# One q unit per step between k and G, tile 4 transposed by DMA, q weights loaded ahead of x of tile 8

## The chip, the core and the metric

The kernel runs on one core of one Trainium2 chip. The metric is the device time of one execution in microseconds (us), lower is better; before the change the median of three runs was 113.4 us, from 112.97 to 113.63 us. A core has five engines with instruction streams of their own: TensorE (PE, matrix products, with the loading of its weights shown apart as PEld), VectorE (DVE), ScalarE (ACT), GpSimd (POOL) and SyncE (SP), which here does nothing but start DMA transfers. Matrix products write into PSUM, which the kernel uses as eight banks of 512 float32 columns.

## The reference

The input x has 2048 rows of 640 values. It is normalised by rows, and three terms are added: x itself, a linear attention with 32 heads of 20 columns, and a small expert block that acts on eight selected rows.

```
xn = (x - mean(x)) / sqrt(var(x) + 1e-5)
q, k, v = split(xn @ wqkv)                      # each 2048 x 640, 32 heads of 20
phi(t) = where(t > 0, t + 1, exp(t)) + 1e-6
kv = phi(k)^T v   and   z = sum of phi(k)       # per head
attention = (phi(q) kv / (phi(q) z)) @ wo
r = xn @ w_r;  idx = the 8 largest of r
expert = (silu(xn[idx] @ w_gate) * (xn[idx] @ w_up)) @ w_down * sigmoid(r[idx])
out = x + attention + xn + scatter(expert at idx)
```

## The kernel before, in words

The rows are cut into 16 tiles of 128. The order of every instruction is the order in which the program emits it; no planner moves anything. Each engine runs its own instructions in that order and waits where an operand isn't ready, so a late operand holds up all that stands behind it on the same engine.

For each tile t the front half of the kernel does the following:

- `stat` computes statistics of two halves of 320 columns on DVE (L180) and merges them (L182). `root_pool` (L191, L192, on POOL) or `root_act` (L186, L187, on ACT) makes the reciprocal root.
- `norm_dve` (L201) or `norm_pool` (L208, L212) writes the normalised tile `xn`.
- The transposed tile `xnT` is made in one of two ways: `tr_pe` transposes on PE with five products (L231), and `tr_ev` copies the result out of banks 7 and 6 with one instruction on ACT (L237) and one on DVE (L242); or `tr_dma` has SP start a transposing DMA (L245). Before, tiles 0 to 4 go by PE and tiles 5 to 15 by DMA.
- `k_half` (L253) multiplies the tile by the k weights, five products of 320 columns per half, into banks 0 and 1 (tiles 1 and 2 use banks 2, 3 and 4, 5). `k_act` (L267, L268) takes exp and relu of both halves on ACT, and one column for the router (L270). `k_phi` (L275, DVE) joins them into `pk`.
- `g1` (L282) adds the tile's part of the matrix G = xn^T phi(k) into banks 2 to 6, five products of 512 columns. It runs four tiles behind k.

The q side works in 20 units, each 128 columns of q for a block of four tiles: `q_mm` (L290, five products of 512 columns, bank 7 unless another is named), `q_act` (L299, L300, ACT), `q_phi` (L306, DVE). `q_ev` is the last two. Units 0 to 4 need tiles 0 to 3, units 5 to 9 need tiles 4 to 7. Units 0 to 7 are spread over the front half by the table `q_at`; the rest fill the back half.

The loads of x, of the q weights `wq` and all DMA transposes are started by SP, in program order, on one queue. The large expert weights are started by ACT in steps 6, 8, 10 and 12 (`w_jobs`, L106). `adds` has POOL scale x for the sum at the end (L480, L223).

After the 16 tiles the router finds its eight rows, G is turned into one matrix M per head group and multiplied into `wo` (`kv_mm`, `m_unit`), the remaining q units run, and `o_mm` (L809) makes the output tile by tile.

Of the kernel before, what the change touches and what calls it, by code (L numbers as in the profile page):

```python
# [36 lines left out]
def kernel(  # L37
# [56 lines left out]
    def load_rest():  # L94

        G.memset(x_sb[0:1, 3, 0:1], 0.0)
        SP.dma_start(x_sb[:, 3, :], x_v[:, 3, :])
        for a in (4, 6):
            SP.dma_start(x_sb[:, a : a + 2, :], x_v[:, a : a + 2, :])
        SP.dma_start(x_sb[:, 8:12, :], x_v[:, 8:12, :])  # L100
        for lo, hi in ((0, 3), (3, 5)):
            SP.dma_start(wq[:, lo:hi, :], wqkv_v[:, lo:hi, 0:D])
        SP.dma_start(x_sb[:, 12:16, :], x_v[:, 12:16, :])
# [158 lines left out]
    def k_act(t):  # L262
        b0 = K_BANK.get(t, 0)
        e = evk.tile([P, 2, HW], BF16, tag="ek", name=f"ek{t}")
        r = evk.tile([P, 2, HW], BF16, tag="rk", name=f"rk{t}")
        for b in range(2):
            A.activation(e[:, b, :], ps[:, b0 + b, 0:HW], AF.Exp)  # L267
            A.activation(r[:, b, :], ps[:, b0 + b, 0:HW], AF.Relu)  # L268
        if t:
            A.copy(r_all[:, t : t + 1], ps[:, b0 + 1, HW : HW + 1])  # L270
        kev[t] = e, r
# [121 lines left out]
    def stats2(t):  # L393
        stat(t, 0)
        stat(t, 1)
# [36 lines left out]
    stats2(4)  # L432
    root_pool(4)
    norm_dve(3)
# [18 lines left out]
    tr_dma(5)  # L453
    norm_pool(6)
    tr_dma(6)
    k_phi(0)
# [3 lines left out]
    q_mm(0)  # L460
    k_phi(2)
    k_half(4, 0)
    q_act(0)
    k_half(4, 1)
    k_act(4)
    k_phi(3)
# [6 lines left out]
    q_phi(0)  # L473
    q_mm(1)
    g1(0)
    k_phi(4)
    q_ev(1)
# [6 lines left out]
    q_at = {5: (2, 3), 6: (4,), 8: (5,), 10: (6,), 12: (7,)}  # L484
    later = {12: [const_grep], 13: [copy_grep]}
    add_at = {7: (0, 1), 9: (1, 1), 11: (2, 1), 12: (3, 2), 13: (5, 2), 14: (7, 3), 15: (10, 3)}
    for t in range(5, T):
        qs = q_at.get(t, ())
# [405 lines left out]
```

## Time and profile before

| | |
|---|---|
| median of three runs | 113.4 us |
| time of the profiled execution | 113.12 us |
| its span in the trace | 111.4 us |
| PE busy | 106.1 us, 95% of the span |
| DVE busy | 81.7 us, 73% |
| ACT busy | 64.9 us, 58% |
| POOL busy | 46.7 us, 42% |
| granted TensorE clock over the span | 0.997 |

The span runs from the first to the last instruction in the trace; 1.7 us of the execution lie around it. A product's shown duration is longer than the pace at which products follow each other, because they are pipelined: a product of 512 columns is shown with 379 ns, and five of them in a row take 1.08 us on the chain. The chain of work that ended last is followed back from the last instruction, so a stretch in which the chain holds only PE rows without a break is one in which PE alone sets the time. In timelines the first column is the start and the second the length, both in us; in rows of DMA issues the last number is the time from issue to landing.

### The profile page before, as it was taken

Reading aid. Unit: us, or ns where it says so; the run is one execution under the profiler, and the core shown is the slowest. Engines: PE = TensorE matmul, PEld = TensorE weight load, DVE = VectorE, ACT = ScalarE, POOL = GpSimd, SP = SyncE. Lnnn points to the kernel's source line nnn. Section 1 sums busy time; section 2 is a strip of 40 time slices with the busy share of each in tenths; the row PEclk is TensorE's granted clock in tenths of the full one; section 3 lists DMA queues with packets and bytes.
Section 4 is the critical chain, followed back from the end, with each engine's and each line's share of the span. In section 5 each row is a group of like instructions: output and inputs, shape, how many; then the busy total and the mean of one; then the engine's idle time right before and its main releaser. Section 6 shows DMA issues by size and latency. Waiting matters only on the chain.

```text
span 111.4 us, 2508 instructions
## 1 busy us (share of the span) xinstructions
PE 106.1 (95%) x911; PEld 62.4 (56%) x911; DVE 81.7 (73%) x176; ACT 64.9 (58%) x165; POOL 46.7 (42%) x93
## 2 busy tenths in 40 slices
PE   5899999999999999999999999999999999999990
PEld 2246544545555555655436879635445566777760
DVE  1799799899997987833829444597788888865670
ACT  1459989597767676766019454478997556300000
POOL 6903578370888689999991331000700000000000
PEclk9999999999999999999999999999999999999998
DMA  3989959502899699799999999927929993333333
GB/s 76 325 260 313 363 198 71 100 15 59 246 295 253 173 178 341 129 397 294 221 315 364 385 381 320 298 81 225 245 16 369 363 328 114 118 121 120 121 118 121
DMA packets 27351, 24.59 MB, mean 221 GB/s; under 512 B 8258, under 2 KB 26058, under 8 KB 27338
## 3 DMA queue, kind: packets, MB, share of 16 engines
q1 hardware_dynamic: 21808, 17.45, 56.1%
q10 hardware_dynamic: 5498, 6.97, 18.8%
q8 instruction: 7, 0.11, 0.5%
q14 instruction: 6, 0.05, 0.2%
q0 software_dynamic: 32, 0.01, 0.1%
HBM read 15.93 MB, written 6.56 MB: 202 GB/s over the span
## 4 chain that ended last, share of the span: by engine, by line
PE 80%; ACT 7%; DVE 3%; POOL 2%; DMA 2%; issue 2%; POOLq 0%; ACTq 0%
PE ps L809 19%; PE ps L290 18%; PE ps L282 14%; PE ps L253 14%; PE ps L528 4%; DMA x_sb<-in_A_x_dram 2%; ACT rq L300 2%; PE ps L650 2%; PE ps L667 2%; PE ps L738 2%; DVE xn L201 1%; PE ps L592 1%; ACT eq L299 1%; ACT ek L267 1%; PE ps L835 1%
## 5 line engine op out<-in xcount | busy, mean ns | idle before, releaser
L253 PE MATMUL ps<-wk,xnT 128*128 128x320 bf16 (+1 forms) x160 | 25.1, 300 | 0.3 <-ACT xnT L237 0.2
L290 PE MATMUL ps<-xnT,wq 128*128 128x512 bf16 x100 | 23.9, 379 | 0.2
L809 PE MATMUL ps<-late,pqT 128*128 128x320 bf16 x150 | 21.3, 299 | 0.0
L253 PEld LDWEIGHTS <-xnT 128*128 128x128 bf16 x160 | 15.2, 97 | 8.5 <-ACT xnT L237 0.8
L282 PE MATMUL ps<-pk,xn 128*128 128x512 bf16 x80 | 19.6, 379 | 0.0
L299 ACT ACTIVATE eq<-ps 128x512 bf16<-128x512 f32 x20 | 11.9, 597 | 11.6 <-PE ps L290 11.6
L275 DVE SCALAR_TENSOR_TENSOR pk<-ek,rk 128x640 bf16<-128x640 bf16 x16 | 14.2, 896 | 5.8 <-ACT rk L268 5.6
L306 DVE SCALAR_TENSOR_TENSOR pqT<-eq,rq 128x512 bf16<-128x512 bf16 x20 | 14.0, 704 | 5.4 <-ACT rq L300 5.4
L809 PEld LDWEIGHTS <-pqT 128*128 128x128 bf16 x150 | 14.3, 98 | 6.2 <-issue 0.4
L267 ACT ACTIVATE ek<-ps 128x320 bf16<-128x320 f32 x32 | 14.5, 453 | 4.5 <-PE ps L253 4.5
L290 PEld LDWEIGHTS <-wq 128*128 128x128 bf16 x100 | 9.3, 98 | 12.3 <-issue 1.5
L818 DVE TENSOR_TENSOR o<-ps,x_sb 128x640 bf16<-128x640 f32 x15 | 12.3, 823 | 5.0 <-PE ps L809 4.6
L180 DVE BATCH_NORM_STATS2 stats<-x_sb 128x6 f32<-128x320 bf16 x32 | 14.3, 479 | 1.8 <-DMA x_sb<-in_A_x_dram 1.8
L223 POOL TENSOR_SCALAR x_sb<-x_sb,rs,nm 128x640 bf16<-128x640 bf16 x13 | 14.9, 1151 | 0.7
L268 ACT ACTIVATE rk<-ps 128x320 bf16<-128x320 f32 x32 | 14.7, 458 | 0.0
L282 PEld LDWEIGHTS <-xn 128*128 128x128 bf16 x80 | 7.6, 98 | 7.6
L300 ACT ACTIVATE rq<-ps 128x512 bf16<-128x512 f32 x20 | 11.9, 593 | 0.0
L191 POOL TENSOR_SCALAR t<-mv 128x1 bf16<-128x1 f32 x9 | 3.8, 427 | 12.5 <-DVE mv L182 12.4
L845 ACT CAST o<-ps 128x160 bf16<-128x160 f32 x1 | 0.3, 293 | 12.7 <-PE ps L835 12.7
L192 POOL TENSOR_TENSOR rs<-t,mhalf 128x1 f32<-128x1 bf16 x9 | 6.8, 760 | 0.7
L618 ACT CAST spare<-ps 128x1024 bf16<-128x1024 f32 (+1 forms) x6 | 4.9, 873 | 3.2 <-PE ps L604 3.2
L781 POOL DMA_INDIRECT s_dram<-y,idx_i x1 | 2.1, 2125 | 9.5 <-DVE late L673 9.5
(127 smaller groups left out, 114.7 us busy)
## 6 DMA issues: line engine op xcount, KB each, us to landing
s_dram<-x_sb SPq DMA_DIRECT2D x4, 640.0 KB, 11.7
x_sb<-s_dram SPq DMA_DIRECT2D x4, 640.0 KB, 6.4
wd<-in_B_w_down_dram SPq DMA_DIRECT2D x1, 1920.0 KB, 13.6
x_sb<-in_A_x_dram SPq DMA_DIRECT2D x2, 640.0 KB, 7.5
rd<-rden ACTq DMA_DIRECT2D x1, 1280.0 KB
spare<-rd SPq DMA_DIRECT2D x2, 640.0 KB, 5.4
out_dram<-o SPq DMA_DIRECT2D x8, 160.0 KB, 1.9
wg<-in_B_w_gate_dram ACTq DMA_DIRECT2D x1, 1152.0 KB, 6.2
```

The source lines that it names most:

```text
L180: V.bn_stats(out=stats[:, t, b, :], in_=x_sb[:, t, b * HW : (b + 1) * HW])
L223: G.tensor_scalar(out=x_sb[:, t, :], in0=x_sb[:, t, :], scalar1=rs1[:, sl], scalar2=nm[:, sl], op0=ALU.mult, op1=ALU.add,)
L253: PE.matmul(ps[:, b0 + b, 0:n], lhsT=xnT[:, kc, t * P : (t + 1) * P], rhs=wk[:, kc, b * HW : b * HW + n], start=(kc == 0), stop=(kc == KC ...
L267: A.activation(e[:, b, :], ps[:, b0 + b, 0:HW], AF.Exp)
L268: A.activation(r[:, b, :], ps[:, b0 + b, 0:HW], AF.Relu)
L275: V.scalar_tensor_tensor(out=pk[:, t, :].rearrange("p (b f) -> p b f", b=2), in0=e[:], scalar=1.0, in1=r[:], op0=ALU.min, op1=ALU.add,)
L282: PE.matmul(ps[:, 2 + c, :], lhsT=xn[:, t, c * P : (c + 1) * P], rhs=pk[:, t, 0:512], start=(t == 0), stop=(t == T - 1),)
L290: PE.matmul(ps[:, bank, :], lhsT=wq[:, kc, m * P : (m + 1) * P], rhs=xnT[:, kc, tb * 512 : (tb + 1) * 512], start=(kc == 0), stop=(kc == K ...
L299: A.activation(e[:], ps[:, bank, :], AF.Exp)
L300: A.activation(r[:], ps[:, bank, :], AF.Relu)
L306: V.scalar_tensor_tensor(out=pqT[:, m, tb * 512 : (tb + 1) * 512], in0=e[:], scalar=1.0, in1=r[:], op0=ALU.min, op1=ALU.add,)
L809: PE.matmul(ps[:, b0 + b, 0:HW], lhsT=pqT[:, kc, t * P : (t + 1) * P], rhs=Ms[:, kc, b * HW : (b + 1) * HW], start=(kc == 0), stop=(kc == ...
```

## The change

The change moves work in the first half of the kernel; the arithmetic of the result stays the same.

- The q weights are loaded by one DMA instead of two, and SP issues it ahead of x of tiles 8 to 11 instead of behind it.
- Tile 3 is normalised between the two statistics halves of tile 4, and not behind both.
- Tile 4 is transposed by DMA. Its five PE products and the two copies go away.
- Ahead of tile 4, PE now does q units 0 and 1 (unit 1 in bank 0) and G of tile 0; of tile 4 the second half comes first, and its bank is emptied first. Unit 2 follows tile 4.
- On DVE `k_phi(0)` stands ahead of the normalisation of tile 5, and tiles 6 and 7 follow it.
- In the loop, steps 6 to 10 have one q unit each, placed between k and G. Before, step 5 had two units and steps 6, 8, 10 and 12 had one, placed ahead of k.
- The reciprocal roots of tiles 9 and 11 move from ACT to POOL.

```diff
         for a in (4, 6):
             SP.dma_start(x_sb[:, a : a + 2, :], x_v[:, a : a + 2, :])
+        SP.dma_start(wq[:], wqkv_v[:, :, 0:D])
         SP.dma_start(x_sb[:, 8:12, :], x_v[:, 8:12, :])
-        for lo, hi in ((0, 3), (3, 5)):
-            SP.dma_start(wq[:, lo:hi, :], wqkv_v[:, lo:hi, 0:D])
         SP.dma_start(x_sb[:, 12:16, :], x_v[:, 12:16, :])
...
-    def k_act(t):
+    def k_act(t, halves=(0, 1)):
...
-        for b in range(2):
+        for b in halves:
...
     k_act(1)
-    stats2(4)
+    stat(4, 0)
+    norm_dve(3)
+    stat(4, 1)
     root_pool(4)
-    norm_dve(3)
     k_half(2, 0)
     tr_pe(3)
...
     norm_dve(4)
+    tr_dma(4)
     stat(5, 1)
     root_pool(5)
     k_half(3, 0)
-    tr_pe(4)
     k_half(3, 1)
-    tr_ev(4, V)
     router_0_out()
     k_act(3)
+    k_phi(0)
+    q_mm(0)
+    norm_dve(5)
+    tr_dma(5)
     stats2(6)
     root_pool(6)
-    norm_dve(5)
-    tr_dma(5)
     norm_pool(6)
     tr_dma(6)
-    k_phi(0)
+    q_act(0)
+    q_mm(1, 0)
+    q_act(1, 0)
     k_phi(1)
     stats2(7)
     root_pool(7)
-    q_mm(0)
+    g1(0)
     k_phi(2)
+    q_phi(0)
+    k_half(4, 1)
     k_half(4, 0)
-    q_act(0)
-    k_half(4, 1)
-    k_act(4)
-    k_phi(3)
+    k_act(4, (1, 0))
+    q_mm(2)
+    q_act(2)
     norm_dve(7)
...
     tr_dma(8)
-    q_phi(0)
-    q_mm(1)
-    g1(0)
+    k_phi(3)
+    q_phi(1)
     k_phi(4)
-    q_ev(1)
+    q_phi(2)
...
-    q_at = {5: (2, 3), 6: (4,), 8: (5,), 10: (6,), 12: (7,)}
+    q_at = {6: 3, 7: 4, 8: 5, 9: 6, 10: 7}
...
-        if qs:
-            q_mm(qs[0])
         k_half(t, 0)
         k_half(t, 1)
         if n < T:
             stats2(n)
+            if n % 2 == 0 or n in (9, 11):
+                root_pool(n)
             if n % 2 == 0:
-                root_pool(n)
                 norm_pool(n)
                 tr_dma(n)
-        if qs:
-            q_ev(qs[0])
         k_act(t)
-        if len(qs) > 1:
-            q_mm(qs[1])
+        if t in q_at:
+            q_mm(q_at[t])
+            q_act(q_at[t])
         g1(t - 4)
         k_phi(t)
-        if len(qs) > 1:
-            q_ev(qs[1])
-        if n < T and n % 2:
+        if t in q_at:
+            q_phi(q_at[t])
+        if 11 < n < T and n % 2:
             root_act(n)
```

More of the change, by code (lines that the diff above doesn't have):

```diff
@@ L482, in adds @@
             add_s(i)
-    q_at = {5: (2, 3), 6: (4,), 8: (5,), 10: (6,), 12: (7,)}
+    q_at = {6: 3, 7: 4, 8: 5, 9: 6, 10: 7}
+    add_at = {7: (0, 1), 9: (1, 1), 11: (2, 1), 12: (3, 2), 13: (5, 2), 14: (7, 3), 15: (10, 3)}
     later = {12: [const_grep], 13: [copy_grep]}
-    add_at = {7: (0, 1), 9: (1, 1), 11: (2, 1), 12: (3, 2), 13: (5, 2), 14: (7, 3), 15: (10, 3)}
     for t in range(5, T):
-        qs = q_at.get(t, ())
         n = t + 4
```

## The prediction

> **What bounds the kernel now.** First the page: PE is busy for nearly the whole span, and the two stretches show where it isn't. In the second fence the columns are the length of the stretch, then busy us and instruction count of PE, PEld, DVE, ACT and POOL, then granted clock, DMA share and GB/s.
>
> ```profile
> PE 106.1 (95%) x911; PEld 62.4 (56%) x911; DVE 81.7 (73%) x176; ACT 64.9 (58%) x165; POOL 46.7 (42%) x93
> ```
>
> ```profile
> 0.00:14.90 14.90, 12.78 (x83) 6.54 (x84) 10.61 (x32) 9.76 (x31) 7.91 (x39) 1.00 0.84 274
> 0.00:16.45 16.45, 14.28 (x91) 7.23 (x92) 12.13 (x36) 11.02 (x34) 9.02 (x41) 1.00 0.79 259
> 24.45:53.30 28.85, 28.85 (x170) 16.47 (x169) 22.16 (x45) 20.58 (x66) 22.09 (x30) 1.00 0.86 231
> ```
>
> From 24.45 to the end of the 16 tiles PE is busy without a break, and on the chain of waits this whole stretch is PE rows. So nothing that only reorders q units after 24.45 can gain; the loop's new table is worth what it saves before 24.45. Two rows of the chain give the paces: ten k products 1.37, five G products 1.08; a q product has the same 512 columns and the same mean as a G product, so five of them take 1.08 too.
>
> ```profile
> 28.13 1.37 PE ps L253 x10
> 29.50 1.08 PE ps L282 x5
> ```
>
> The breaks stand in PE's own timeline before that (start, length; the length holds the last product's tail, so I go by starts and paces).
>
> ```profile
> 10.54 0.85 PE L253 MATMUL ps<-wk,xnT 128*128 128x320 bf16 x5
> 11.46 0.45 PE L231 MATMUL ps<-ident,xn 128*128 128x128 bf16 x5
> 11.75 1.53 PE L253 MATMUL ps<-wk,xnT 128*128 128x321 bf16 x10
> 13.36 0.45 PE L231 MATMUL ps<-ident,xn 128*128 128x128 bf16 x5
> 13.65 0.85 PE L253 MATMUL ps<-wk,xnT 128*128 128x321 bf16 x5
> 15.81 1.53 PE L253 MATMUL ps<-wk,xnT 128*128 128x320 bf16 x10
> 18.25 1.24 PE L282 MATMUL ps<-pk,xn 128*128 128x512 bf16 x5
> 19.59 1.24 PE L290 MATMUL ps<-xnT,wq 128*128 128x512 bf16 x5
> 23.11 1.24 PE L282 MATMUL ps<-pk,xn 128*128 128x512 bf16 x5
> 24.45 0.38 PE L290 MATMUL ps<-xnT,wq 128*128 128x512 bf16 x1
> ```
>
> G of tile 0 ends at 18.25 + 1.08 = 19.33 and the next q unit starts at 19.59: 0.26 lost on bank 7, which ACT has not emptied. The same at 24.45: 23.11 + 1.08 = 24.19, 0.26 lost. Earlier, 0.24 before 11.46 and 0.24 before 13.36 (both waits for a normalised tile), 0.29 of tile 4's transposes (13.36 to 13.65), and 0.39 around q unit 0, which waits for its weights (13.65 + 0.69 = 14.34 to 15.81, less 1.08). Together about 1.7 us: all that this change can win.
>
> **The change part by part.**
>
> *q weights ahead of tile 8.* The rows are SP's issues (start, length), then the landings of the DMAs issued at 6.71, 7.78 and 8.31.
>
> ```profile
> 6.71 0.47 SPq L100 DMA_DIRECT2D x_sb<-in_A_x_dram  x1
> 7.78 0.49 SPq L102 DMA_DIRECT2D wq<-in_A_wqkv_dram  x1
> 8.31 0.52 SPq L103 DMA_DIRECT2D x_sb<-in_A_x_dram  x1
> ```
>
> ```profile
> x_sb<-in_A_x_dram SPq DMA_DIRECT2D x1, 640.0 KB, 6.4
> wq<-in_A_wqkv_dram SPq DMA_DIRECT2D x1, 320.0 KB, 7.5
> x_sb<-in_A_x_dram SPq DMA_DIRECT2D x1, 640.0 KB, 8.6
> ```
>
> Tile 8's load lands at 13.1, the q weights (800 KB in all) at 15.3, the last x load at 16.9. Swapped, the weights take tile 8's place plus 160 KB; 800 KB took 2.2 us behind it, so they land near 13.1 + 0.4 = 13.5. Tiles 8 to 11 then land at 15.3, and their statistics start after 20: no cost. The last load still lands at 16.9, the bytes being the same.
>
> *Tile 3 between the halves.* PE can start its transposes when k's half ends, 10.54 + 0.69 = 11.23, instead of 11.46. But ACT's copy of the result stands behind its work on tile 1 and starts at 11.84 either way, having no idle time before it:
>
> ```profile
> 11.84 0.48 ACT L237 COPY xnT<-ps 128x384 bf16<-128x384 bf16 x1
> ```
>
> So k of tile 3 starts near 12.36 (before: 11.75 + 0.69 = 12.44). Without tile 4's transposes its ten products end at 12.36 + 1.37 = 13.73, q unit 0 at 14.81, q unit 1 at 15.89 (bank 0: ACT, without the tile 4 copy of 0.48, has emptied it by 14.6), G of tile 0 at 16.97. Up to here all is gain.
>
> *Tile 4 by DMA.* Its normalisation is bound by POOL's root and stays where it is, so SP issues the transpose at about 13.35. Behind it SP holds only the transposes of tiles 5 and later.
>
> ```profile
> 12.86 0.44 DVE L201 TENSOR_SCALAR xn<-x_sb,mv,rs 128x640 bf16<-128x640 bf16 x1 [0.22 <-POOL rs L192]
> ```
>
> Now the landing. Three transposes of before, issued at these times, landed 4.2, 4.3 and 2.6 us later:
>
> ```profile
> 15.52 1.32 SPq L245 DMA_TRANSPOSE xnT<-xn  x1
> 36.09 1.20 SPq L245 DMA_TRANSPOSE xnT<-xn  x1
> 24.53 1.20 SPq L245 DMA_TRANSPOSE xnT<-xn  x1
> ```
>
> ```profile
> xnT<-xn SPq DMA_TRANSPOSE x1, 4.2
> xnT<-xn SPq DMA_TRANSPOSE x1, 4.3
> xnT<-xn SPq DMA_TRANSPOSE x1, 2.6
> ```
>
> The lower end of its landing is 13.35 + 2.6 = 15.95, if nothing stands before it. But on SP's queue two x loads of 640 KB do, until 16.9. That small transfers there wait for large ones is shown by three of 40 KB that took 9.7 us, issued right behind `wo`, which took up to 11.0:
>
> ```profile
> grep<-grep SPq DMA_DIRECT2D x3, 40.0 KB, 9.7
> wo<-in_A_wo_dram SPq DMA_DIRECT2D x1, 500.0 KB, 11.0
> ```
>
> The loads' data ends near 16.5, 0.4 before the landing. Of the 2.6 of a free transpose 1.2 is SP's issue, so 1.4 is left: 16.5 + 1.4 = 17.9. What made 4.2 of the one at 15.52? In a window of 0.2 us around 16.5 the queue of instruction fetches moved one packet of 16 KB, and around 38.05, where the one of 4.3 was in flight, another; the page counts seven such packets in all.
>
> ```profile
> q8 instruction: 1, 0.02, 46.7%
> q8 instruction: 1, 0.02, 23.7%
> q8 instruction: 7, 0.11, 0.5%
> ```
>
> Seven for 911 products and 911 weight loads: they are PE's. The transpose at 24.53, beside no such packet, took 2.6. So a fetch costs the transpose in flight 1.6 or 1.7. (If the loads and not the fetch had held the one at 15.52, tile 4 would stand behind the same loads and land no earlier than it did, 19.7.) PE had started between 83 and 91 products when it was asked for (the fence with 14.90 and 16.45, if it was taken up between these loads). In the changed order the 83rd product is the second of unit 1, near 15.1, and the 91st the last of G of tile 0, near 16.9: the fetch again falls on a tile that waits behind the loads, only that now this is tile 4, for which PE waits. I take 17.9 + 1.7 = 19.6; the upper end counts from the last load's landing instead of its data, 16.9 + 1.4 + 1.7 = 20.0.
>
> [...]
>
> *The sum.* k of tile 4 starts 0.05 after the landing, 19.65, and ends at 21.02. PE has then done what it had done at 19.33 before: 1.69 later. The two breaks of 0.26 go: q unit 2 finds bank 7 free, and in steps 6 to 10 a unit and G, 2.16 together, stand between k and the next use of its banks. 1.69 - 0.52 = +1.17. From there PE runs without a break as before, so the end moves by the same: 113.12 + 1.17 = 114.3 for the profiled execution, and 113.4 + 1.17 = 114.6 for the median, which stands 0.28 above it.
>
> *The rest, at nothing, with its cover.* `k_phi(0)` ahead of tile 5 costs DVE 0.78, against 0.28 saved; tile 5's DMA still goes out near 15.4 and lands behind tile 4's, one transpose (about 1.0) later, 20.6 to 21.7; its k starts at 19.65 + 2.44 = 22.1. Tile 6 goes out about 1.2 later (19.3), lands near 22 and is wanted at 24.5. Roots of tiles 9 and 11 on POOL (1.2 to 1.5 each) delay only scalings of x that are read much later. The load jobs on ACT now stand behind `q_act`, about 1.1 later, and in step 10 `wu` goes out shortly after tile 13's transpose and can hold it until its own end. These rows of before are ACT's issue, the time to landing, and tile 13's k.
>
> ```profile
> 39.04 0.37 ACTq L106 DMA_DIRECT2D wu<-in_B_w_up_dram  x1
> wu<-in_B_w_up_dram ACTq DMA_DIRECT2D x1, 1152.0 KB, 5.6
> 45.88 1.53 PE L253 MATMUL ps<-wk,xnT 128*128 128x320 bf16 x10
> ```
>
> The load ended 1.2 before that k; 1.1 later leaves 0.1. If that cover goes, it costs up to 0.5.
>
> **The rivals.**
>
> 1. *The fetch misses tile 4, or costs nothing* (other side). Landing 17.9, k at 17.95: 17.95 + 1.37 - 19.33 - 0.52 = -0.53, so 112.9. It decides at a landing of 18.43; earlier than that the kernel gets faster. For it: the transpose at 24.53. Against it: the packet near 16.5, which would have to come over 1 us later.
> 2. *Tile 4 isn't held by the loads at all.* Landing 15.95, PE never waits: 16.97 + 1.37 - 19.33 - 0.52 = -1.51, so 111.9. The 40 KB rows speak against it.
> 3. *PE falls back to a slow clock while it waits.* In the main case it idles 19.65 - 16.97 = 2.7 us; before, its longest break after the start was under 0.4. The first products of the kernel ran slow, 594 ns shown against 379 for the same shape:
>
> ```profile
> L151 PE MATMUL ps<-zw 128*128 128x512 bf16 x10 | 4.3, 594 | 1.2 <-DVE zw L139 1.2
> L290 PE MATMUL ps<-xnT,wq 128*128 128x512 bf16 x100 | 23.9, 379 | 0.2
> ```
>
> Nine again at twice the pace would cost 9 x 0.215 = 1.9: 116.5. [...]
>
> **How the numbers follow.** Main case 0.66, rival 1 0.17, rival 2 0.06, rival 3 0.08, others 0.03. Prediction 114.6; the main case alone, by landings of 19.3 to 20.0, is 114.3 to 115.0, and 115.5 with the 0.5 of tile 13. The range takes in rival 1 and leaves out 2 and 3: 112.8 to 115.5. This kernel can tell 0.5% (0.57 us) from no change; rival 1 stands on that bound and is split, and a main case with an early landing (18 to 19) is no change: faster 0.2, same 0.12, slower 0.68.
>
> **What would show it.** Right: PE idle for about 2.7 us ahead of k of tile 4, released by the DMA of `xnT`; its landing 6 us or more after the issue; an instruction packet between 15 and 18; no break at 19.6 or 24.4 of the old kind. Wrong: tile 4 lands before 18.4, or PE is late elsewhere, above all at k of tile 5 or tile 13, or slow products follow the wait.

## The result, and the profile after

The changed kernel takes 116.46 us (median of four runs, 116.23 to 117.51) against 113.28 for the kernel before on the same chip: a ratio of 1.030, 95% interval 1.023 to 1.037. It is slower by about 3.2 us; forecast was 1.2 slower, with 115.5 as the upper end. The profiled execution took 116.23 us with a span of 114.5, 3.1 more than before. Where single runs of a kernel lie more than 1.5% above its fastest, its ratio and interval leave them out while its median holds them, so that a ratio isn't always the quotient of two medians.

First the page of the changed kernel: busy time, the TensorE clock in 40 slices, the shares of the chain that ended last.

```profile
PE 106.4 (93%) x906; PEld 62.6 (55%) x906; DVE 80.3 (70%) x175; ACT 64.2 (56%) x160; POOL 49.1 (43%) x97
...
PEclk9999999679999999999999999999999999999999
...
PE 81%; DMA 8%; DVE 4%; ACT 2%; POOL 1%; issue 1%; POOLq 0%; ACTq 0%
```

PE's busy time is the same as before (106.1), although five transposes are gone, and the share fell: the kernel waits more. Two slices between 20 and 26 us show a clock of 0.6 and 0.7, where the page before has 0.9 or more in every slice but the last. The chain now holds DMA for 8% of the span (2% before).

The router's first transpose on PE follows G's last part of the 16 tiles, so its start marks the end of the front half; here it is in PE's timeline of the kernel before (start, length).

```profile
53.31 0.22 PE L535 MATMUL ps<-ident,r_all 128*16 128x128 bf16 x1
```

The same row in PE's timeline of the changed kernel:

```profile
56.34 0.22 PE L535 MATMUL ps<-ident,r_all 128*16 128x128 bf16 x1
```

The front half ends 3.03 later, so it holds all but 0.1 of the loss; behind it 58.1 and 58.2 us follow. Where the 3.03 arise, PE's timeline of the changed kernel shows (in brackets the idle time before the row and what ended it).

```profile
14.39 2.33 PE L289 MATMUL ps<-xnT,wq 128*128 128x512 bf16 x10 [0.54 <-DMA wq<-in_A_wqkv_dram]
16.56 1.24 PE L281 MATMUL ps<-pk,xn 128*128 128x512 bf16 x5
19.82 1.76 PE L252 MATMUL ps<-wk,xnT 128*128 128x321 bf16 x10 [2.02 <-DMA xnT<-xn]
21.38 2.34 PE L289 MATMUL ps<-xnT,wq 128*128 128x512 bf16 x5
23.51 1.98 PE L252 MATMUL ps<-wk,xnT 128*128 128x320 bf16 x10
...
26.40 1.53 PE L252 MATMUL ps<-wk,xnT 128*128 128x320 bf16 x10
```

k of tile 4 starts at 19.82, held by its transpose (landed 19.78, forecast 19.6). By the prediction's own count (k's 1.37, less the old 19.33, less two breaks of 0.52) this is 19.82 + 1.37 - 19.33 - 0.52 = 1.34 of loss. Then from the start of k of tile 4 to that of tile 5 pass 3.69 us instead of 2.44 (ten k products and a q unit), and from there to tile 6 2.89 instead of 2.45: 1.69 in all. 1.34 + 1.69 = 3.03, the whole loss of this execution. The windows name the 1.69 (length, then busy us and count of PE, PEld, DVE, ACT and POOL, granted clock, DMA share, GB/s):

```profile
17.59:21.00 3.41, 1.39 (x10) 0.86 (x10) 2.35 (x6) 0.53 (x2) 3.02 (x5) 1.00 0.84 64
21.00:24.41 3.41, 3.41 (x12) 1.44 (x11) 2.66 (x7) 1.96 (x7) 1.63 (x4) 0.50 0.48 96
24.41:27.82 3.41, 3.41 (x24) 2.14 (x23) 3.25 (x9) 2.47 (x8) 3.01 (x5) 1.00 0.02 5
```

For 3.41 us after PE's wait the granted clock was 0.50, and PE started 12 products where the next stretch of the same length has 24. Half of 3.41 is 1.7: the prediction's rival 3. But that is the account of one execution only, and the first experiment shows that it isn't the account of the others.

### The profile page after: what moved, and what is told of

Read it like the earlier page. It is cut to its first block, busy times and chain, and to the rows that moved or that the text cites. A ratio compares the mean times of both kernels' runs of the same rounds, so it can differ in the third digit from the quotient of the medians.

```text
span 114.5 us, 2505 instructions
## 1 busy us (share of the span) xinstructions
PE 106.4 (93%) x906; PEld 62.6 (55%) x906; DVE 80.3 (70%) x175; ACT 64.2 (56%) x160; POOL 49.1 (43%) x97
## 4 chain that ended last, share of the span: by engine, by line
PE 81%; DMA 8%; DVE 4%; ACT 2%; POOL 1%; issue 1%; POOLq 0%; ACTq 0%
PE ps L289 18%; PE ps L809 18%; PE ps L252 15%; PE ps L281 14%; DMA xnT<-xn 6%; PE ps L528 4%; DMA x_sb<-in_A_x_dram 2%; DVE xn L200 2%; PE ps L650 2%; PE ps L667 2%; DVE stats L179 2%; PE ps L738 2%; PE ps L592 1%; PE ps L835 1%; PE ps L679 1%; POOL rs L191 1%
## 5 line engine op out<-in xcount | busy, mean ns | idle before, releaser
L289 PE MATMUL ps<-xnT,wq 128*128 128x512 bf16 x100 | 24.7, 392 | 0.5 <-DMA wq<-in_A_wqkv_dram 0.5
L281 PE MATMUL ps<-pk,xn 128*128 128x512 bf16 x80 | 19.6, 379 | 0.0
L274 DVE SCALAR_TENSOR_TENSOR pk<-ek,rk 128x640 bf16<-128x640 bf16 x16 | 13.7, 854 | 6.7 <-ACT rk L267 6.7
L222 POOL TENSOR_SCALAR x_sb<-x_sb,rs,nm 128x640 bf16<-128x640 bf16 x13 | 13.0, 1005 | 0.7
L190 POOL TENSOR_SCALAR t<-mv 128x1 bf16<-128x1 f32 x11 | 6.1, 557 | 12.9 <-DVE mv L181 12.5
L191 POOL TENSOR_TENSOR rs<-t,mhalf 128x1 f32<-128x1 bf16 x11 | 8.4, 762 | 0.9
L200 DVE TENSOR_SCALAR xn<-x_sb,mv,rs 128x640 bf16<-128x640 bf16 x11 | 4.9, 450 | 4.9 <-POOL rs L191 4.4
```

What stands on the lines that cost most here:

```text
L222: G.tensor_scalar(out=x_sb[:, t, :], in0=x_sb[:, t, :], scalar1=rs1[:, sl], scalar2=nm[:, sl], op0=ALU.mult, op1=ALU.add,)
L274: V.scalar_tensor_tensor(out=pk[:, t, :].rearrange("p (b f) -> p b f", b=2), in0=e[:], scalar=1.0, in1=r[:], op0=ALU.min, op1=ALU.add,)
L281: PE.matmul(ps[:, 2 + c, :], lhsT=xn[:, t, c * P : (c + 1) * P], rhs=pk[:, t, 0:512], start=(t == 0), stop=(t == T - 1),)
L289: PE.matmul(ps[:, bank, :], lhsT=wq[:, kc, m * P : (m + 1) * P], rhs=xnT[:, kc, tb * 512 : (tb + 1) * 512], start=(kc == 0), stop=(kc == K ...
```

## The experiments

My theory at the start: the wait for tile 4 costs about 1.3 and the half clock behind it 1.7. The rival: something else in the new order costs the 1.7, and the half clock only hides it. Four kernels run together on one chip: the changed kernel once more, and three that each take away the wait or the slow clock in another way.

**a_again: the changed kernel, unchanged.**

> The changed kernel once more, for its trace and the granted clock of each run. Theory (late tile, then slow clock): the transpose of tile 4 lands 6 us or more after its issue, PE waits about 2 us, and where the clock is granted at half afterwards it lasts one stretch of 3.4 us and costs 1.7 us: 116.2 to 116.8 with it. Runs with a clock of 1.000 should then be near 114.8. Rival (the slow clock is chance and not the price): runs with a clock of 1.000 are as slow, 116.2 or more, and their trace shows the time elsewhere.

116.74 us, ratio 1.025 (1.014 to 1.036). Its profiled execution (116.52) has the same wait of PE and no half clock behind it: in the windows of this kernel PE is busy for the same 1.39 us, and then the clock stays whole.

```profile
17.59:21.00 3.41, 1.39 (x10) 0.80 (x9) 2.35 (x6) 0.53 (x2) 3.02 (x5) 1.00 0.82 64
21.00:24.41 3.41, 3.41 (x23) 1.97 (x21) 2.66 (x7) 3.15 (x10) 1.63 (x4) 1.00 0.48 96
```

And yet it is no faster. In its place another wait stands in PE's timeline, at tile 8:

```profile
19.92 1.54 PE L252 MATMUL ps<-wk,xnT 128*128 128x321 bf16 x10 [2.02 <-DMA xnT<-xn]
33.11 1.54 PE L252 MATMUL ps<-wk,xnT 128*128 128x320 bf16 x10 [1.08 <-DMA xnT<-xn]
```

k of tile 7 started at 28.35; a k, a q unit and G later, 3.52, tile 8 was due at 31.87 and started at 33.11: 1.24 lost. With 19.92 + 1.37 - 19.33 - 0.52 = 1.44 that is 2.68 of the 2.73 by which this front half ends later (56.04).

In the execution with half clock k of tile 8 started at 33.45, later than here, but without waiting. The first load of the expert weights `wg` is the difference. ACT's timeline of the changed kernel, in the execution with half clock:

```profile
29.06 0.40 ACTq L105 DMA_DIRECT2D wg<-in_B_w_gate_dram  x1
```

ACT's timeline of a_again:

```profile
27.48 0.41 ACTq L105 DMA_DIRECT2D wg<-in_B_w_gate_dram  x1
```

The slow products held up ACT, which works on their results, and with it this load. Tile 8's transpose, issued at 26.88 in both executions, landed at 29.44 with half clock; in a_again it landed at 33.06, 0.6 ahead of the end of `wg` (33.70). So either loss is there, and the half clock stands in for the hold at tile 8. The four runs of the changed kernel agree: two have a clock of 0.985 over their span, which is what one stretch of 3.41 us at 0.50 gives, and took 116.23 and 117.51; the two at 0.998 and 1.000 took 116.50 and 116.42. The rival is right: with a whole clock the time is the same and is lost elsewhere.

**a_fill: nine idle products in the wait for tile 4, so that the clock stays whole.**

```diff
     q_phi(0)
+    warm(9, 1)
     k_half(4, 1)
```

> The changed kernel with nine idle products of 512 columns (zeros into bank 1, which k of tile 4 then overwrites) between G of tile 0 and k of tile 4, so that PE is busy for about 1.9 us of its wait. The landing of tile 4 stays as it is. Theory (slow clock from the wait): no stretch of half clock, 1.7 us less than the changed kernel: 114.8 and still slower than before by 1.2%. Rival (the wait alone costs 3 us, or the clock isn't tied to it): 116.2 or more.

117.04 us, ratio 1.029 (1.021 to 1.037); no gain. The clock was 1.00 throughout. This kernel's chain of waits (start, length) at tile 8:

```profile
27.19 6.25 DMA xnT<-xn
33.44 0.05 issue
33.49 1.54 PE ps L252 x10
```

Its DMA issues between 26.6 and 29 us, the last number being the time to landing:

```profile
wg<-in_B_w_gate_dram ACTq DMA_DIRECT2D x1, 1152.0 KB, 5.8
xnT<-xn SPq DMA_TRANSPOSE x1, 6.2
```

ACT's timeline there:

```profile
27.05 0.39 ACTq L105 DMA_DIRECT2D wg<-in_B_w_gate_dram  x1
```

And PE's timeline, in a view that ends at 34 us:

```profile
33.49 0.72 PE L252 MATMUL ps<-wk,xnT 128*128 128x320 bf16 x4 [1.88 <-DMA xnT<-xn]
```

ACT issued the first 1152 KB of `wg` at 27.05 and it landed 5.8 later, at 32.8; tile 8's transpose, issued at 27.19, landed at 33.44, 0.6 behind it. Before, tile 8 went out at 24.53 (a row of the prediction), ahead of `wg`, and landed in 2.6. k of tile 7 started at 27.92 here, so tile 8 lost 33.49 - 31.44 = 2.05. With tile 4's 19.50 + 1.37 - 19.85 = 1.02 and 0.58 at tile 15, held by `wu` in the same way, this makes 3.65 of 3.67.

**a_x12late: x of tiles 12 to 15 loaded behind tile 4's transpose instead of ahead of it.**

```diff
-        SP.dma_start(x_sb[:, 12:16, :], x_v[:, 12:16, :])
...
     tr_dma(4)
+    SP.dma_start(x_sb[:, 12:16, :], x_v[:, 12:16, :])
     stat(5, 1)
```

> The changed kernel with the load of x of tiles 12 to 15 issued by SP behind the transpose of tile 4 and not ahead of it; nothing else differs. Theory (tile 4 waits behind loads on SP's queue): the transpose has only the load of tiles 8 to 11 before it, lands at 17 to 18 and not at 19.8, k of tile 4 starts at 17.6 to 18.1, no half clock: 112.4 to 113.0. Rival (a transpose at this place takes 6 us whatever stands before it, or the q order costs the time): 115 or more.

116.75 us, ratio 1.029 (1.019 to 1.038). SP's issue of tile 4's transpose in this kernel:

```profile
13.47 1.32 SPq L243 DMA_TRANSPOSE xnT<-xn  x1
```

Its time to landing among the DMA issues:

```profile
xnT<-xn SPq DMA_TRANSPOSE x1, 2.7
```

And k of tiles 4 and 5 in PE's timeline:

```profile
17.00 1.53 PE L251 MATMUL ps<-wk,xnT 128*128 128x321 bf16 x10
...
20.74 1.54 PE L251 MATMUL ps<-wk,xnT 128*128 128x320 bf16 x10 [1.14 <-ACT rq L298]
```

Without that load ahead of it tile 4 landed in 2.7 instead of 6.4, and PE didn't wait for it. That alone doesn't name the load as the cause, because the packet on the queue of instruction fetches came at 16.46 here, behind tile 4's landing at 16.17. Tile 5 does: issued at 16.02, now behind the load, it landed at 20.70, 0.6 after the load (20.11) and long after that packet. So a load ahead on SP's own queue held this transpose, as the prediction had it. The gain was gone by tile 8 again: PE took tile 5 up at 20.74 (the row names ACT, which had long been done), tile 6 landed at 23.39 and was taken up at 23.44, and tile 8, held by `wg`, landed at 32.51.

**a_tr4pe: tile 4 back on PE, all else as changed.**

```diff
     norm_dve(4)
-    tr_dma(4)
     stat(5, 1)
     root_pool(5)
     k_half(3, 0)
+    tr_pe(4)
     k_half(3, 1)
+    tr_ev(4, V)
```

> The changed kernel with tile 4 transposed on PE again, as in the kernel before; the other parts of the change stay. Theory (all of the loss is tile 4's DMA): G of tile 0 ends near 17.6, k of tile 4 follows without a wait, both breaks of 0.26 go: 0.85 less than before, 112.4. Rival (q between k and G, or the early q units, cost something themselves): 113.3 or more.

116.66 us, ratio 1.027 (1.018 to 1.036). k of tile 4 started at 18.20 without a wait, and then PE's timeline of this kernel has (the view ends at 34 us):

```profile
23.89 1.54 PE L252 MATMUL ps<-wk,xnT 128*128 128x320 bf16 x10 [0.63 <-DMA xnT<-xn]
...
33.01 1.26 PE L252 MATMUL ps<-wk,xnT 128*128 128x320 bf16 x8 [1.90 <-DMA xnT<-xn]
```

Tile 6's transpose was issued at 21.27 and landed 2.57 later, so no load held it; it went out late. Tile 8's, issued at 27.40, landed at 32.96. So even the piece of the change that the prediction counts as its whole cost can be taken back without any gain: three waits stand one behind another, at tile 4, tile 6 and tile 8, and who passes the first arrives at the next.

Why tiles 6 and 8 go out late, DVE and POOL show. DVE's timeline of the kernel before, with the statistics of tile 6 and the scaling of tile 7:

```profile
14.06 0.87 DVE L180 BATCH_NORM_STATS2 stats<-x_sb 128x6 f32<-128x320 bf16 x2
...
19.94 0.45 DVE L201 TENSOR_SCALAR xn<-x_sb,mv,rs 128x640 bf16<-128x640 bf16 x1 [0.46 <-POOL rs L192]
```

POOL's timeline of the kernel before, with the start of the roots of tiles 6 and 7:

```profile
15.27 0.30 POOL L191 TENSOR_SCALAR t<-mv 128x1 bf16<-128x1 f32 x1 [0.36 <-DVE mv L182]
...
18.16 0.67 POOL L191 TENSOR_SCALAR t<-mv 128x1 bf16<-128x1 f32 x1
```

DVE's timeline of the changed kernel, with the scaling of tile 5, the statistics of tile 6 and the scaling of tile 7:

```profile
15.47 0.45 DVE L200 TENSOR_SCALAR xn<-x_sb,mv,rs 128x640 bf16<-128x640 bf16 x1 [0.77 <-POOL rs L191]
15.83 0.88 DVE L179 BATCH_NORM_STATS2 stats<-x_sb 128x6 f32<-128x320 bf16 x2
...
21.71 0.45 DVE L200 TENSOR_SCALAR xn<-x_sb,mv,rs 128x640 bf16<-128x640 bf16 x1 [1.74 <-POOL rs L191]
```

POOL's timeline of the changed kernel, the same two roots:

```profile
17.04 0.68 POOL L190 TENSOR_SCALAR t<-mv 128x1 bf16<-128x1 f32 x1 [1.61 <-DVE mv L181]
...
20.80 0.23 POOL L190 TENSOR_SCALAR t<-mv 128x1 bf16<-128x1 f32 x1
```

Before, DVE made tile 6's statistics (14.06) ahead of scaling tile 5, while POOL worked out tile 5's root. In the new order `k_phi(0)` and scaling tile 5 stand first: DVE waits 0.77 for that root, and tile 6's statistics start at 15.83, 1.77 later. POOL then idles 1.61 (0.36 before) and starts tile 6's root at 17.04 instead of 15.27. From there to tile 7's root POOL's own work for tile 6 takes 3.76 instead of 2.89 (why its instructions are longer, no run shows), so that root starts at 20.80 instead of 18.16, 2.64 later, and DVE waits 1.74 for it. From there each tile inherits the lateness. SP's timeline of the kernel before, tile 6:

```profile
18.10 1.20 SPq L245 DMA_TRANSPOSE xnT<-xn  x1
```

SP's timeline of the changed kernel, tiles 6 and 8:

```profile
20.74 1.20 SPq L244 DMA_TRANSPOSE xnT<-xn  x1
...
26.88 1.20 SPq L244 DMA_TRANSPOSE xnT<-xn  x1
```

2.64 and 2.35 later. The first load of `wg` doesn't follow DVE and POOL. It follows PE: in the new table ACT issues it 2.65 or 2.66 after the start of k of tile 6, in every profile of it with the loads in their old steps; before, it was 1.58. That gave 27.10 before, 27.05 in a_fill and 27.48 in a_again: with a whole clock the load stayed where it was, while tile 8 went out over 2 us later.

**b_phi0: that order of DVE alone, in the kernel before.**

```diff
-    stats2(6)
-    root_pool(6)
+    k_phi(0)
     norm_dve(5)
     tr_dma(5)
+    stats2(6)
+    root_pool(6)
     norm_pool(6)
     tr_dma(6)
-    k_phi(0)
```

> The kernel before with one part of the change: phi of tile 0 on DVE ahead of the normalisation of tile 5, which is ahead of the statistics of tile 6, as in the changed kernel. New theory (this order makes POOL's roots and the scalings of tiles 6 to 8 late): the transpose of tile 8 goes out about 1.4 us later than 24.5, near 26; if it is then caught by the wg load, k of tile 8 starts at 33.1 instead of 31.5 and the time is 115.0; if it just slips through, 113.4 to 113.8. Rival (the lateness comes from the other parts): tile 8 goes out at 24.5 to 25 and the time is 113.4.

115.75 us (115.02 to 116.82), ratio 1.016 (1.008 to 1.023). A new order of a few lines, which touches no product and no load, costs about 1.8 us by this ratio. Its profiled execution is the longest of its runs, so I take no sum from it. POOL starts the roots of tiles 6 and 7 at 17.11 and 21.01, as in the changed kernel (17.04 and 20.80), so this order by itself makes that lateness. Tile 8 goes out at 26.51 instead of 24.53. Here it slips in 1.3 ahead of `wg` (27.84); tiles 10 and 13 are caught instead, and PE waits for both.

**a_tr4pe_phi0: the reverse. Tile 4 on PE, and DVE's old order around tile 6.**

```diff
     k_act(3)
-    k_phi(0)
     q_mm(0)
-    norm_dve(5)
-    tr_dma(5)
     stats2(6)
     root_pool(6)
+    norm_dve(5)
+    tr_dma(5)
     norm_pool(6)
     tr_dma(6)
+    k_phi(0)
     q_act(0)
```

(and tile 4 as in a_tr4pe)

> The changed kernel with tile 4 on PE and with the order of the kernel before on DVE in one place: statistics of tile 6, then the normalisation of tile 5, and phi of tile 0 behind the scaling of tile 6. Theory (phi of tile 0 ahead makes the chain of tiles 5 to 8 late): the transpose of tile 8 goes out near 25 instead of 27.4, slips ahead of wg and lands before 28.5; no tile waits up to tile 8, k of tile 8 starts near 30.7 instead of 33.0: 113.6 to 114.4. Rival (the lateness is the q order's own): 116 or more, tile 8 issued after 26.5.

115.55 us, ratio 1.013 (1.004 to 1.022), 1.1 less than a_tr4pe. In the profiled execution, again the longest of its runs, tile 6 goes out at 18.18, and its k starts at 22.54 without a wait. Tile 8 goes out at 25.05, still 0.5 later than before, and `wg`, issued at 25.2, lands at 31.4: the transpose at 31.19. A head start of 0.15 wasn't enough to pass, and neither was one of 0.60 in a_again.

The front half of this execution ends 0.90 later than before (54.21), its span is 3.1 longer. The rest is lost behind the front half, where PE's timeline has a wait for POOL's copies of the eight selected rows, `xsT`:

```profile
73.49 1.00 PE L739 MATMUL ps<-wg,xsT 128*32 128x384 bf16 x20 [1.95 <-POOL xsT L582]
```

The profiled executions of the kernel before and of the changed kernel don't wait there. Eight of the eighteen others do, by 0.4 to 2.0 us, because POOL first loads the number of each row: these eight loads took 0.86 to 1.49 us each here, and 0.29 to 0.99 in the kernel before. What makes them longer, no run shows. So totals of these kernels compare less well than their front halves.

**b_loop: the loop's new table alone, in the kernel before.**

```diff
-    q_at = {5: (2, 3), 6: (4,), 8: (5,), 10: (6,), 12: (7,)}
+    q_at = {5: 2, 6: 3, 7: 4, 8: 5, 9: 6, 10: 7}
...
-        qs = q_at.get(t, ())
...
-        if qs:
-            q_mm(qs[0])
...
-        if qs:
-            q_ev(qs[0])
         k_act(t)
-        if len(qs) > 1:
-            q_mm(qs[1])
+        if t in q_at:
+            q_mm(q_at[t])
+            q_act(q_at[t])
         g1(t - 4)
         k_phi(t)
-        if len(qs) > 1:
-            q_ev(qs[1])
+        if t in q_at:
+            q_phi(q_at[t])
```

> The kernel before with the loop's new table alone: units 2 to 7 in steps 5 to 10, one per step, between k and G; all ahead of step 5, the roots and the loads stay. Theory (the table saves the break of 0.26 ahead of 24.45 and the one at 19.59, and the DVE chain stays in time): 112.9 to 113.4. Rival (q between k and G delays DVE's work for the next tiles, and the transposes with it): transposes of tiles 9 to 13 go out 1 us or more later than before, 114.5 or more.

114.22 us, ratio 1.005 (1.000 to 1.009): it wins nothing. Its front half ends at 53.60, 0.29 later than before: PE came to tile 4 0.26 later in this execution, and lost 0.50 at tile 15, whose transpose ran beside the second `wu`.

**b_wq: the q weights ahead of x of tile 8 alone, in the kernel before.**

```diff
+        SP.dma_start(wq[:], wqkv_v[:, :, 0:D])
         SP.dma_start(x_sb[:, 8:12, :], x_v[:, 8:12, :])
-        for lo, hi in ((0, 3), (3, 5)):
-            SP.dma_start(wq[:, lo:hi, :], wqkv_v[:, lo:hi, 0:D])
```

> The kernel before with one part of the change alone: the q weights in one load, issued ahead of x of tiles 8 to 11; no result changes. If this part costs nothing, as the prediction has it, q unit 0 starts at 14.34 and its five products follow each other, PE gains the 0.39 us lost there, tile 5 still lands before its k (20.7 less 0.4), and the kernel takes 113.0 to 113.4 with the front half ending near 52.9. Rival: the later x of tiles 8 to 11 delays statistics and transposes on DVE and POOL, a transpose meets the wg load (tile 8 issued later than 25.5), and the kernel takes 114.5 or more.

113.30 us against 113.58, ratio 0.999 (0.995 to 1.002): no difference that can be measured. Its front half ends at 53.08, 0.23 earlier. This part is innocent, as the prediction had it.

**The expert loads.** If the loads catch the transposes, then other places for the loads should help. Three trials of this missed.

*a_tr4pe_chunk, a_chunk, b_chunk: `wg` and `wu` in ten pieces of 384 KB, one per step from 5 to 14*, in a_tr4pe, the changed kernel and the kernel before.

```diff
-        6: [lambda: kcw(wg, B_w_gate, 0, 3)], 8: [lambda: kcw(wg, B_w_gate, 3, 5)],
-        10: [lambda: kcw(wu, B_w_up, 0, 3)], 12: [lambda: kcw(wu, B_w_up, 3, 5)],
...
+    for i in range(2 * KC):
+        w, src = ((wg, B_w_gate), (wu, B_w_up))[i // KC]
+        w_jobs.setdefault(5 + i, []).insert(0, lambda w=w, src=src, k=i % KC: kcw(w, src, k, k + 1))
...
-    w_jobs[14] = [lambda: load_wd(0, FC)]
+    w_jobs.setdefault(14, []).append(lambda: load_wd(0, FC))
```

> The kernel with tile 4 on PE again, and besides the loads of the expert weights wg and wu cut into ten pieces of 384 KB, one per step from 5 to 14, instead of four of 1152 and 768 KB in steps 6, 8, 10 and 12. New theory (the transpose of tile 8 goes out after 26.5 instead of 24.5 and is then held by the large wg load until 33): no transpose is held for more than about 1.2 us, k of tile 8 starts near 31 instead of 33.0, about 2.1 us less: 114.4. Rival (k of tile 8 is late for another reason, the order of the q units or DVE): still 116 or more.

> The changed kernel with only the loads of wg and wu cut into ten pieces, as above. New theory: k of tile 8 no longer waits for wg. Where the clock stays whole after the wait for tile 4 it starts near 31.9 instead of 33.1, 115.2 in all; where it is halved for 3.4 us, nothing is gained, 116.4, because PE then comes to tile 8 late anyway. Rival: no run under 116.

> The kernel before with only the loads of wg and wu cut into ten pieces, as a control. There tile 8 lands at 27.1, before wg starts, and tile 9 lands 0.85 us ahead of its k: nothing waits, so cutting gains nothing: 113.4, within 0.5%. If the cutting itself costs or gains, this run shows by how much.

117.51 us, ratio 1.032 (1.025 to 1.038); 119.31 (116.78 to 120.33, too scattered for a ratio); 114.73, ratio 1.007 (1.003 to 1.012). None gained; that cutting costs by itself is shown for the kernel before alone, 0.7%. In a_tr4pe_chunk tile 8 is no longer held (issued 26.83, landed 29.88), but tiles 12 and 14 are, and PE waits 1.31 and 1.26 for them. The smaller pieces took the wait from one tile and gave it to others.

*a_tr4pe_phi0_jobs, a_jobs, a_fill_jobs: the four loads a step or two later*, at 7, 9, 11 and 14, in a_tr4pe_phi0, the changed kernel and a_fill.

```diff
-        6: [lambda: kcw(wg, B_w_gate, 0, 3)], 8: [lambda: kcw(wg, B_w_gate, 3, 5)],
-        10: [lambda: kcw(wu, B_w_up, 0, 3)], 12: [lambda: kcw(wu, B_w_up, 3, 5)],
-        13: [lambda: load_cols(wv, 0, KC, 2 * D), load_wo],
+        7: [lambda: kcw(wg, B_w_gate, 0, 3)], 9: [lambda: kcw(wg, B_w_gate, 3, 5)],
+        11: [lambda: kcw(wu, B_w_up, 0, 3)], 13: [lambda: load_cols(wv, 0, KC, 2 * D), load_wo],
...
-    w_jobs[14] = [lambda: load_wd(0, FC)]
+    w_jobs[14] = [lambda: kcw(wu, B_w_up, 3, 5), lambda: load_wd(0, FC)]
```

> Tile 4 on PE, DVE order of before around tile 6, the q table of the change, and the four loads of wg and wu, in their old sizes, moved to steps 7, 9, 11 and 14, one step behind the pairs of transposes. Theory (the loads' collisions are what is left): the transposes of tiles 8 and 9 take under 3 us, k of tile 8 starts near 29.6 instead of 31.2, the front half ends near 52.5: 112.6, faster than before by 0.7%. Rival (another tile is then caught, 10, 12 or 14): the wait only moves, 113.5 to 115.

> The changed kernel with only the four loads moved to steps 7, 9, 11 and 14. Theory (tile 4's wait is 1.2 us, the rest was either half clock or tile 8 behind wg): with a whole clock k of tile 8 starts near 31.9 and the time is 114.8 to 115.2; with half clock 116.2 to 116.5. Rival (the loads are not the cause): 116.2 or more with a whole clock too.

> As the run above, with the nine idle products in PE's wait for tile 4, so that the clock can't fall. Theory: both ways of losing the further 1.2 to 1.7 us are shut, no run with half clock, 114.6 to 115.0, which is the forecast's main term alone. Rival: 116 or more.

116.33 (ratio 1.011, 1.006 to 1.017), 117.64 (1.036, 1.032 to 1.041) and 117.64 (1.035, 1.029 to 1.041). Tile 8 is free in all three (landed 2.6 after its issue), and tile 14 is caught in all three, by the first load of `wu`. The profiled execution of a_jobs had the half clock too, 3.41 us from 20.78 on, and lost about 1.9 at tile 14 besides. In PE's timeline of a_fill_jobs:

```profile
51.54 1.54 PE L251 MATMUL ps<-wk,xnT 128*128 128x320 bf16 x10 [1.69 <-DMA xnT<-xn]
```

*a_late, b_late: all four loads at step 15*, so that no transpose meets them, in the changed kernel and in the kernel before.

```diff
-        6: [lambda: kcw(wg, B_w_gate, 0, 3)], 8: [lambda: kcw(wg, B_w_gate, 3, 5)],
-        10: [lambda: kcw(wu, B_w_up, 0, 3)], 12: [lambda: kcw(wu, B_w_up, 3, 5)],
+        15: [lambda: kcw(wg, B_w_gate, 0, 3), lambda: kcw(wg, B_w_gate, 3, 5),
+             lambda: kcw(wu, B_w_up, 0, 3), lambda: kcw(wu, B_w_up, 3, 5)],
```

> The changed kernel with the four loads of wg and wu moved behind step 15, so that no load of ACT's queue meets a transpose. They may make the second half late, so the front half is read from the trace: the start of the router's transpose, 53.3 before and 56.3 in the changed kernel. Theory (transposes that go out 2 us later are held by these loads): after tile 4 no tile waits, none of the transposes of tiles 8 to 13 takes over 4 us, and the front half ends near 54.6 with a whole clock (56.3 with half clock for 3.4 us). Rival (the front half is late for another reason): 56 or more with a whole clock.

> The kernel before with the same four loads behind step 15, as the control of the run above. No tile waited for them before, so the front half ends at 53.3 as before; whatever the time rises by is the price of the late loads in the second half, which the run above pays too. Both theories expect the same here.

123.10 (ratio 1.084, 1.079 to 1.089) and 117.17 (1.033, 1.027 to 1.039): the back half now waits for the late loads, so only the front halves can be compared. They end at 54.82 and 53.58. The profiled execution of a_late is the longest of its runs, so it only hints: from tile 7 on every transpose lands 2.6 after its issue and PE waits for none of them; tile 4 is early (k at 17.85) and tile 6 late (1.96 of wait).

**a_fill_late and a_tr4pe_late: the cleanest pair.** a_fill with the loads at step 15 takes away the half clock and the loads and keeps tile 4's wait; a_tr4pe with the loads at step 15 takes away tile 4's wait and the loads and keeps the late order of DVE.

```diff
-        6: [lambda: kcw(wg, B_w_gate, 0, 3)], 8: [lambda: kcw(wg, B_w_gate, 3, 5)],
-        10: [lambda: kcw(wu, B_w_up, 0, 3)], 12: [lambda: kcw(wu, B_w_up, 3, 5)],
+        15: [lambda: kcw(wg, B_w_gate, 0, 3), lambda: kcw(wg, B_w_gate, 3, 5),
+             lambda: kcw(wu, B_w_up, 0, 3), lambda: kcw(wu, B_w_up, 3, 5)],
...
     q_phi(0)
+    warm(9, 1)
     k_half(4, 1)
```

(a_tr4pe_late has a_tr4pe's edit in the place of the second part)

> The changed kernel with nine idle products in PE's wait for tile 4 (so that the clock stays whole) and with the four expert loads at step 15 (so that no transpose meets them); no result changes. Theory (the whole loss is the forecast's wait for tile 4, the half clock, and transposes held by loads, with the half clock and the holds standing in for each other): k of tile 4 near 19.5, no wait of PE after it, the front half ends at 53.58 + 1.0 = 54.6 us (53.58 is the kernel before with the same late loads), total near 118.2. Rival (the later order on DVE and POOL costs by itself, without any load): PE waits at tile 6, 8 or later by 0.5 us or more each, and the front half ends at 55.5 or later.

> The changed kernel with tile 4 back on PE and the four expert loads at step 15. Theory: of its losses with the loads in place, 2.07 at tile 8 and 0.15 at tile 13 fall away, 0.8 at tile 6 stays because that transpose goes out late whatever the loads do; the front half ends near 56.08 - 2.2 = 53.9 us, total near 117.5. Rival (lateness alone): transposes land 2.6 us after their issue and PE still waits at tile 8, front half at 55.5 or later.

123.19 (ratio 1.079, 1.071 to 1.088) and 123.60 (1.084, 1.075 to 1.092), 5 us and more above what I had expected of the totals: the load of `wd` now runs beside the four others (in a_fill_late it was issued at 52.53 and landed at 75.45, and ACT waited 9.6 us for it), as I had not counted. The front halves are what was asked. The profiled execution of a_fill_late is the longest of its runs; its half clock, 10.24 us from 72.70 on, lies in the back half, and up to 50 us the clock was whole. Two windows of it:

```profile
0.00:25.00 25.00, 22.32 (x134) 11.84 (x137) 17.85 (x47) 16.06 (x48) 14.06 (x47) 1.00 0.78 198
25.00:50.00 25.00, 24.89 (x145) 14.17 (x146) 21.08 (x47) 18.09 (x54) 20.82 (x29) 1.00 0.27 54
```

The landing of tile 8 (issued at 27.04) among its DMA issues:

```profile
xnT<-xn SPq DMA_TRANSPOSE x1, 2.6
```

And the router's first transpose in its PE timeline:

```profile
54.19 0.22 PE L536 MATMUL ps<-ident,r_all 128*16 128x128 bf16 x1
```

k of tile 4 started at 19.35 here: 19.35 + 1.37 - 19.33 - 0.52 = 0.87, and the front half ends 54.19 - 53.31 = 0.88 later than before. With half clock and loads out of the way the prediction's sum, from the measured start of tile 4 on, holds to 0.01 us, and the rest of the new order costs nothing beside the wait for tile 4. (Against b_late, the kernel before with the same late loads, the front half ends 0.61 later; there k of tile 4 had itself started 0.27 later than in the kernel before.) No run confirms the sum on the total time: in every kernel of the new order with the loads in the front half PE lost time at a later tile too, or to the clock. a_tr4pe_late ends its front half at 53.57: 0.26 later than before although it doesn't wait at tile 4; it loses 0.3 or less each at tiles 6, 12 and 14.

All starts side by side (us; "ahead" is by how much tile 8's transpose was issued ahead of the first load of `wg`; "clock" is the lowest granted clock between 20 and 28 us; units between the tiles are ordered otherwise in the first row, so its k of tile 6 and 8 are not compared with the others):

| kernel | k of tile 4 | k of tile 6 | ahead | k of tile 8 | front half ends | clock |
|---|---|---|---|---|---|---|
| before | 15.81 | 25.52 | 2.57 | 31.49 | 53.31 | 1.0 |
| changed | 19.82 | 26.40 | 2.18 | 33.45 | 56.34 | 0.5 |
| a_again | 19.92 | 24.82 | 0.60 | 33.11 (held by `wg`) | 56.04 | 1.0 |
| a_fill | 19.50 | 24.40 | -0.14 | 33.49 (held by `wg`) | 56.98 | 1.0 |
| a_x12late | 17.00 | 23.44 (late) | -0.87 | 32.55 (held by `wg`) | 56.60 | 1.0 |
| a_tr4pe | 18.20 | 23.89 (late) | -0.85 | 33.01 (held by `wg`) | 56.08 | 1.0 |
| a_tr4pe_phi0 | 17.65 | 22.54 | 0.14 | 31.24 (held by `wg`) | 54.21 | 1.0 |
| a_fill_late | 19.35 | 24.25 | no load | 31.30 | 54.19 | 1.0 |
| a_tr4pe_late | 18.09 | 23.32 (late) | no load | 30.38 | 53.57 | 1.0 |

In the five rows from "changed" to a_tr4pe tile 4 starts anywhere from 17.0 to 19.9, and tile 8 within 32.6 to 33.5. What was won at tile 4 was gone by tile 8: tile 6 goes out late whatever tile 4 does, and where PE comes to tile 6 earlier it brings `wg` forward as well, against a tile 8 that stays where it was. In the last three rows the order on DVE or the loads are others, and tile 8 starts 1.2 us and more earlier.

No variant beat the kernel before; b_wq equals it.

## Why the prediction was wrong

The direction was right and the size wrong: 1.2 us forecast, 3.2 measured, above the range.

*q weights ahead of tile 8, at nothing.* Right in cost: b_wq alone changes nothing that can be measured. Their landing was 14.34 and not 13.5 (PE's first q unit starts at 14.39, after a break of 0.54), but this delay lies inside the time that PE would have waited for tile 4.

*Tile 3 between the halves.* Nearly as forecast: its transposes start at 11.32 (11.23), and k of tile 3 is ready when q unit 0 isn't.

*Tile 4 by DMA.* Right in both causes, and near in the number with some luck: issued at 13.39 (13.35), landed at 19.78 (19.6), but the load ahead landed at 17.82 and not at 16.9, and the tile 1.96 behind it and not 2.7. That a load ahead held a transpose, a_x12late shows (tile 5, landed 0.6 behind the load). A packet on the queue of instruction fetches started at 17.71 while tile 4's transpose was in flight. The prediction took these packets for PE's, and they do start with PE's products: of the seven, six start within three products of the same count before and after (92 and 91 products for the first, 211 and 211 for the second, at 16.50 and 17.71 and at 38.05 and 41.77 us), the fourth does not (478 and 502). That a transpose beside such a packet landed late without a large load, b_late shows: with the expert loads out of the way, tile 12 was issued at 36.36 and would have landed near 39.0 if it had taken 2.6 like others of that run. The queue of instruction fetches in the 0.1 us from 38.3 on, and this tile's time to landing, both in b_late:

```profile
q8 instruction: 1, 0.02, 70.6%
```

```profile
xnT<-xn SPq DMA_TRANSPOSE x1, 4.4
```

1.8 more than 2.6, near the 1.6 or 1.7 of the prediction. How the 6.4 of tile 4 divides between load and fetch stays open: in a_late, with load and packet at 17.1, the tile landed 0.7 behind both.

*The sum.* 1.17 forecast, 1.34 in the profiled execution; and 0.87 by the same formula against 0.88 measured in a_fill_late, where nothing else interferes. "From there PE runs without a break as before" is the sentence that didn't hold: with half clock PE had no break but ran at half pace for 3.41 us, and with a whole clock it had a break at tile 8.

*"The rest, at nothing, with its cover."* This is the step that failed. It put tile 6 at 19.3 (20.74 measured), asked whether its k would wait, found that it wouldn't, and stopped there. Two mistakes lie in it. The delay was too small: 2.64 instead of 1.2. Of this 1.77 came through DVE, where the wait for tile 5's root wasn't counted, and 0.87 through POOL's work for tile 6, which took longer than before. And a lateness on DVE and POOL isn't used up at the tile where it arises: tiles 8 to 15 go out later as well, against loads of ACT that follow PE. I had looked for such a meeting at tile 13 and `wu` alone, with a price of up to 0.5; it came at tile 8 and `wg`, at 1.2 to 2.1, because the kernel before had tile 8 out only 2.6 us ahead of `wg` (24.53 against 27.1). The prediction's 1.1 for ACT's loads behind `q_act` was right (2.66 instead of 1.58 after k of tile 6), but it was set against tile 13 only.

*Rival 3, the slow clock.* Priced at 1.9, it came at 1.69 in the profiled execution, and I had given it 0.08. It isn't the cause by itself either: where the clock stays whole, tile 8's wait takes its place. At tile 8 the two are alternatives and not a sum, because the half clock sent `wg` out later (29.06 instead of 27.48 in a_again).

*Rivals 1 and 2.* Both would have needed tile 4 before 18.4. a_x12late got that (16.17) and was no faster: the outcome didn't hang on tile 4 alone.

*The loop's new table*, taken as worth 0.52 at best, gained nothing alone (b_loop). Within the whole change the 0.52 does come in, as the agreement of 0.87 and 0.88 shows.

What stays open: why POOL's instructions for tile 6 took longer in the new order, and why a transpose issued beside a large load of another queue landed only near that load's end. That it did, the landings show (33.44 against 32.8 in a_fill, 31.19 against 31.4 in a_tr4pe_phi0). In the changed kernel tile 9 was held for 6.2 us without PE waiting for it, so being held cost only where the slack was gone.

## What to carry to other kernels

When an engine off the critical path gets a new order, follow the delay through every later tile and ask at each one which transfer of another queue it now runs beside; here the delay arose at tiles 5 and 6, and tile 8 paid the most. Before scaling by a root that another engine still computes, give the waiting engine the next tile's statistics: the other order alone cost 1.6% here (b_phi0). And a loss can stand in for another one: taking one wait away tells nothing of its price until the next wait behind it is known, so look at where each run's front stands at a few fixed marks rather than at its total.

## What the hardware showed that I had not expected

The half clock came after a short wait. In the changed kernel PE waited 2.02 us ahead of k of tile 4; the 3.41 us from 21.00 on ran at 0.50, and in the stretch of the same length before them PE was busy for 1.39. a_again had the same wait of 2.02 and the same 1.39 busy us in the same place, and its next 3.41 us ran at 1.00. So a wait of 2 us cost 1.7 us in one execution and left the clock whole in another; what decides it, no run here shows.

A transposing DMA of one tile took 2.6 us from issue to landing with no load in flight beside it (tile 8 before, issued at 24.53), and 6.2 beside a 1152 KB load that another engine issued (tile 9 before, issued at 26.91; `wg` at 27.10). At tile 8 a head start of 0.60 us on such a load was not enough (a_again) and one of 2.18 was (the changed kernel). Beside a packet of 16 KB on the queue of instruction fetches it took 4.4 without any such load (tile 12 in b_late). Smaller loads were no cure: with ten pieces of 384 KB PE still waited 1.31 and 1.26 us, at tiles 12 and 14 (a_tr4pe_chunk).
